# Products of zeros in TensorE's waits, from the attention's end to the first gather

## The chip, the core and the metric

The kernel runs on one core of a Trainium2 chip. A core has TensorE (PE, with its weight loads shown apart as PEld), VectorE (DVE), ScalarE (ACT), GpSimd (POOL) and SyncE (SP), which issues transfers. Each engine executes its own instructions in order, and semaphores tie the engines together. The metric is the device time of one execution in microseconds. TensorE's clock has two levels, 1.2 and 2.4 GHz; the profile gives the granted clock as a share, 0.50 or 1.00.

## The reference

Causal attention by blocks of 64 over 8 batches, 8 heads, 576 positions of width 64; then a layer of 8 experts, in which each of the 4608 tokens goes to one expert and each expert takes 576; then a dense layer with the activation h cos(h).

```python
attn = softmax(mask(q @ k.T / 8)) ; x = (attn @ v) as 4608 x 512
logits = x @ w_gate                       # 4608 x 8
for idx in argsort(-logits.flatten()):    # best pair of token and expert first
    tok, e = idx // 8, idx % 8
    if token unassigned and counts[e] < 576: assigned[tok] = e
for e: out[assigned == e] = relu(x[mask] @ w1[e]) @ w2[e]
h = out @ w_in ; result = (h * cos(h)) @ w_out
```

## The kernel before

`attention` runs first: 64 heads in a software pipeline whose order on TensorE is written out by hand. It leaves the rows `xs` in HBM and the gate's logits `lg` in SBUF. Then `moe` takes the experts one after another. The greedy assignment is replayed without a sort: the expert that fills up first is found, with the value of its last token.

For the first of them nothing else can run yet, so this search is on the path. `search_pe` (L776 to L804) finds the threshold four bits at a time, in eight rounds. In a round VectorE compares each token's best logit with 16 thresholds (`compare`, `cm`, L774), in four pieces of 7, 9, 10 and 10 tiles; TensorE counts by expert in 36 products of 8 columns, one a tile (L787); VectorE compares the counts with the capacity (`fl`, L789); one product with `W16` (L792) tells all partitions; and VectorE makes the next thresholds (L801, L803). Then `close` (L862 on) ranks the tokens of the expert: running sums and two products (L880, L881), one-hot matrices (`om`, `B`, `hot`, L891 to L903), 36 products that place the token numbers (L913) and one that spreads them (L921). The result is `idx` (L928), which GpSimd uses to gather the rows in five indirect transfers (`xg`, L938).

`begin` and `xpose` start the first expert's products. `xpose` transposes a gathered tile on TensorE (L1013), ScalarE rounds it to `xth` (L1018), VectorE takes the rest, `xtl` (L1019). For the second tile both go in two halves, and the second half's `xth` waits for the first half's `xtl`. TensorE's first products (L1190) need both tiles. Meanwhile `load_raw` brings weights `wr`; the fourth to sixth are held until gathers have landed, by a one-element copy on VectorE (L972). ScalarE turns them into `wh` (L979), VectorE into `wl` (L980). The claims of the second expert (L702 to L737: `sel`, `e`, `oh`, `w`, `cmp`, `cmw`, `ri`, `rj`, `rd`) run on VectorE at the same time.

The order of TensorE and VectorE is that of the program while the first search and close run; after that TensorE's is still that of the program, and the other engines' is set by a scheduler's model of costs. `wu` is a tile of zeros; products of it go into accumulators that nobody reads. Before, 14 of them (`warm`, L855) stand behind L921; transposes of `xg` whose result isn't read (L1022) follow the first two real ones.

Of the kernel before, what the change touches and what calls it, by code (L numbers as in the profile page):

```python
# [19 lines left out]
F32 = mybir.dt.float32  # L20
# [15 lines left out]
NT = 36  # L36
# [5 lines left out]
PR = dict(EC=3, E2=2, E5=7, GC=0, SI=1, NX=3, LV=3, Q0=2, WM=14, WE=0, SW=1, W0=16, WG=0, WN=5, PA=0, CS=2, sT=2, mx=3, tr=1, e32=3, RO=0, XO=0, SO=0, GO=200, TPS=4, SEP=5, L2=3, L5=9, LAG=3, WK=3, XG=5, BIG=16, GLD=99, IW=4, W1=14, CW=1, XS=6, AH=3)  # L42
# [11 lines left out]
def attention(ctx, tc, qk, vv, vt, cmask, wg, xs, lg, ident, wu, side, late):  # L54
# [5 lines left out]
    nc = tc.nc  # L60
# [4 lines left out]
    P = ctx.enter_context(tc.tile_pool(name="at_ps", bufs=1, space=PSUM))  # L65
# [386 lines left out]
    for g in range(NHD + 2):  # L452
        p, h = divmod(g, 2)
        b, pr = divmod(p, 4)
        on = g < NHD
        if on and b + 1 < B and g % 8 == (5 if b == 0 else PR["LV"]):
            if b == 0:
                hold(VB[1][0:1, 0, 0, 0:1])
                hold(VB[1][0:1, 4, 0, 0:1])
            load_v(b + 1)  # L460
        if g == 0:
            start()
            continue
        if on and h == 0 and p + 1 < NP:
            if p == 2:
                hold(VT[1][0:1, 0:1])
            load_vt(p + 1)
        if on and h == 0:
            if p > 1 and p + 3 < NP:
                load_max(p + 3)  # L470
            if p == 1:
                zero(0, nc.gpsimd)
                mask(0)
            if p > 3 and p + 2 < NP:
                load_raw(p + 2)
        work = side(g)
        gms = [x for x in MX.get(g, [g + 4]) if x < NHD]

        def m(u):
            for x in gms:  # L480
                mx_unit(x, u)

        def s(t):
            if on:
                sc_unit(g, t)

        def a(j):
            if 0 <= g - 1 < NHD:
                av_part(g - 1, j)

        def c():
            if h == 0 and 1 < p + 1 < NP and p != 1:
                crow(p + 1)

        def x1():
            if 0 <= g - 2 < NHD:
                sums(g - 2)

        def x2():
            if 0 <= g - 2 < NHD:  # L500
                norm(g - 2)
            if g % 8 == 2 and g > 2:
                store_x(b - 1)

        more = on and 0 < p and p + 1 < NP

        def rc():
            if more:
                copies(p + 1, h)

        def rd():
            if more:
                rests(p + 1, 0)

        def rp():
            if more:
                rests(p + 1, 1)

        def v():
            q = p + 1 if h == 1 and p + 1 < NP else None  # L520
            if q is not None:
                for j in range(5):
                    vg_unit(q, j)

        def k():
            for x in gms:
                if x % 2:
                    crow_max(x // 2)

        def V():  # L530
            for j in range(5):
                vg_unit(1, j)

        did = {"P0": lambda: rest_pair(1, 0), "P1": lambda: rest_pair(1, 1), "L3": lambda: load_max(3), "L4": lambda: load_max(4),
               "R0": lambda: row_part(1, 0, 4, 1), "R1": lambda: row_part(1, 4, 5, 1), "Y0": lambda: copies(1, 0), "Y1": lambda: copies(1, 1),
               "T0": lambda: round_pair(2, 0), "T1": lambda: round_pair(2, 1), "X0": lambda: head_max(0, NM[1]), "X1": lambda: head_max(1, NM[1]), "Z": lambda: zeros(2, nc.gpsimd), "Z1": fourth, "H6": lambda: load_raw(5), "C1": lambda: crow(1), "C": lambda: crow(2),
               "H": held, "H4": later_pair, "V": V, "x1": x1, "x2": x2, "c": c, "rc": rc, "rd": rd, "rp": rp, "v": v, "k": k}
        order = ORDER[h]
        if 0 < g < 4:
            order = (FIRST, SECOND, THIRD)[g - 1]  # L540
        if g == 6:
            order = order.replace(" c ", " c H6 ")
        if g > 59:
            order = LATE if g == 60 else LATE.replace("rd rp ", "")
            if g >= NHD:
                order = "x1 a0 a1 x2 D a2 a3 a4"
        for w in order.split():
            if w in did:
                did[w]()
            elif w[0] in "ABD":  # L550
                for f in work.pop(w[0], ()):
                    f()
            elif w[0] == "M":
                mx_unit(int(w[1]), int(w[2]))
            elif w[0] == "G":
                vg_unit(0, int(w[1]))
            elif w[0] in "sam" and len(w) == 2:
                {"s": s, "a": a, "m": m}[w[0]](int(w[1]))
        for w in work.values():
            for f in w:  # L560
                f()
        if g > 5:
            late()
    first.close()
    opening.close()
    store_x(B - 1)
# [115 lines left out]
def moe(ctx, tc, ro, xs, hs, lg, w1h, w2h, winh, wouth, out, ident, jp):  # L682
    nc=tc.nc
    C=ctx.enter_context(tc.tile_pool(name="mo_c",bufs=1))
    W=ctx.enter_context(tc.tile_pool(name="mo_w",bufs=2))
    P=ctx.enter_context(tc.tile_pool(name="mo_ps",bufs=4,space=PSUM))
# [3 lines left out]
    hp, asg, oh, w4, mc, sel, eid, idx, wu, e2 = (ro.hp, ro.asg, ro.oh, ro.w4, ro.mc, ro.sel, ro.eid, ro.idx, ro.wu, ro.e2)  # L690
# [70 lines left out]
    def last_base(je):  # L761

        jf=R.tile([128,1],F32,name="jf",bufs=1); f8=R.tile([128,8],F32,name="f8",bufs=1)
        V.tensor_reduce(jf,je,axis=AX.X,op=OP.max)
        V.scalar_tensor_tensor(f8,je,jf,rev8,op0=OP.is_equal,op1=OP.mult)
        fm=first(f8)
        V.tensor_scalar(jj,jf,-1.0,None,op0=OP.add)
        V.tensor_tensor(bx,bx,jj,op=OP.bitwise_xor)
        return fm
# [5 lines left out]
    def search_pe():  # L775
        for l in range(8):  # L776
            sh=28-4*l
            if l>0: compare(l,((0,7),(7,16),(16,26),(26,36)),th)
            cm=CM[l]
            if l>0: V.tensor_tensor(bx,bx,jj,op=OP.bitwise_xor)  # L780
            if l==2:
                XG[0,0]=W.tile([128,512],F32,name="xg",bufs=PR['XG'])
                G.indirect_dma_start(out=XG[0,0][0:16],out_offset=None,in_=xs,in_offset=bass.IndirectOffsetOnAxis(ap=T8[0:16,1,0:1],axis=0))
            yield
            ps=psum()
            for t in range(NT):
                nc.tensor.matmul(ps[0:16,0:8],lhsT=cm[:,t,:],rhs=oh[:,t,:],start=t==0,stop=t==NT-1)  # L787
            fl=R.tile([16,8],BF,name="fl")
            V.tensor_scalar(fl,ps[0:16,0:8],float(CAP),None,op0=OP.is_ge)  # L789
            yield  # L790
            ps2=psum()
            nc.tensor.matmul(ps2[:,0:8],lhsT=W16[:,l],rhs=fl,start=True,stop=True)  # L792
            if l==7: return last_base(ps2[:,0:8])
            if l==0:

                jf=R.tile([128,1],F32,name="jf",bufs=1)
                V.tensor_reduce(jf,ps2[:,0:8],axis=AX.X,op=OP.max)
                V.tensor_scalar(jj,jf,-float(1<<31),None,op0=OP.add)
                V.tensor_scalar(bx,jj,31,0x7FFFFFFF,op0=OP.arith_shift_right,op1=OP.bitwise_and)
            else:  # L800
                V.tensor_reduce(jj,ps2[:,0:8],axis=AX.X,op=OP.max)  # L801
            t2=R.tile([128,16],I32,name="th",bufs=2)
            V.scalar_tensor_tensor(t2,TS[:,l+1],jj[:,0:1],bx.to_broadcast([128,16]),op0=OP.bitwise_xor,op1=OP.bitwise_xor)  # L803
            th=t2.bitcast(F32)  # L804
# [43 lines left out]
        V.scalar_tensor_tensor(f8,ps[:,0:8],float(CAP),rev8,op0=OP.is_ge,op1=OP.mult)  # L848
        return first(f8)

    def warm(a,n):

        for _ in range(n):
            ps=P.tile([128,512],F32,name="acc",bufs=4)
            nc.tensor.matmul(ps[0:64],lhsT=a,rhs=wu,start=True,stop=True)  # L855

    sn=R.tile([128,1],F32,name="sn",bufs=1)
    XG={}
# [3 lines left out]
    def close(i,fm):  # L862
# [16 lines left out]
        ps=psum()  # L879
        nc.tensor.matmul(ps[:,0:72],lhsT=LT,rhs=g2f,start=True,stop=False)  # L880
        nc.tensor.matmul(ps[:,0:72],lhsT=ones,rhs=gs,start=False,stop=True)  # L881
        if i==0: warm(gs[:,0:64],PR['WE'])
        yield
        a2=R.tile([128,2,NT],F32,name="a2",bufs=1); pp=R.tile([128,NT],I32,name="pp",bufs=1); pi=R.tile([128,NT],I32,name="pi",bufs=1)
        V.scalar_tensor_tensor(a2,ps[:,0:72].rearrange("p (a t) -> p a t",a=2),-5000.0,g2,op0=OP.add,op1=OP.mult)
# [13 lines left out]
        hot=[]  # L899
# [11 lines left out]
        ps=psum()  # L911
        for t in range(NT):
            nc.tensor.matmul(ps[0:18,0:64],lhsT=B[:,t].rearrange("p s m -> p (s m)"),rhs=hot[t//9][:,t%9],start=t==0,stop=t==NT-1)  # L913
        yield
        pr=R.tile([18,2,64],BF,name="pr",bufs=1)
        V.tensor_copy(pr,ps[0:18,0:64].unsqueeze(1).to_broadcast([18,2,64]))
# [2 lines left out]
            yield from bank()  # L919
        ps=psum()  # L920
        nc.tensor.matmul(ps[:,0:9],lhsT=pr.rearrange("p h r -> p (h r)"),rhs=both,start=True,stop=True)  # L921
        if i==0: warm(hot[3][:,8],PR['WM'])
        yield
        m0=(CAP*i)//128; r0=9*i%2
        for h in range(2):

            c=(9*i+(h^r0))//2; b=h^r0; k=(10-b)//2
# [7 lines left out]
        for j in range(5):  # L935
            n=64 if (j==4 and i%2==0) else 128
# [201 lines left out]
    a,b,c=steps[-3:]  # L1138
# [178 lines left out]
```

## Time and profile before

| | |
|---|---|
| median of 3 runs | 1686.72 us (1684.54 to 1686.97) |
| the profiled execution | 1680.93 us |
| its span, first to last instruction | 1679.1 us |
| TensorE busy | 1655.2 us, 99% of the span |
| VectorE, ScalarE busy | 1084.7 us (65%), 808.7 us (48%) |
| mean granted clock | 0.990 |

Times in rows are microseconds from the span's start unless marked ns. A row of a timeline gives start, length, engine, line, operation, what is written and read, and in brackets the idle time before it and what ended that.

### The profile page before, as it was taken

Reading aid. Unit: us, or ns where it says so; the run is one execution under the profiler, and the core shown is the slowest. Engines: PE = TensorE matmul, PEld = TensorE weight load, DVE = VectorE, ACT = ScalarE, POOL = GpSimd, SP = SyncE. Lnnn points to the kernel's source line nnn. Section 1 sums busy time; section 2 is a strip of 40 time slices with the busy share of each in tenths; the row PEclk is TensorE's granted clock in tenths of the full one; section 3 lists DMA queues with packets and bytes.
Section 4 is the critical chain, followed back from the end, with each engine's and each line's share of the span. In section 5 each row is a group of like instructions: output and inputs, shape, how many; then the busy total and the mean of one; then the engine's idle time right before and its main releaser. Section 6 shows DMA issues by size and latency. Waiting matters only on the chain.

```text
span 1679.1 us, 29288 instructions
## 1 busy us (share of the span) xinstructions
PE 1655.2 (99%) x10852; PEld 1478.6 (88%) x10852; DVE 1084.7 (65%) x2896; ACT 808.7 (48%) x1622; POOL 294.2 (18%) x259
## 2 busy tenths in 40 slices
PE   9999999998899999999999999999999999999998
PEld 8999999997698898899889889988988988998887
DVE  6888888887769777676667667677554343433342
ACT  6566666664345634443442544344254344434443
POOL 7344443432124400100100100100110000000000
PEclk9999999998799999999999999999999999999999
DMA  8999999995442323323433423433433333323332
GB/s 165 284 231 230 245 251 241 235 206 181 144 155 107 120 95 108 122 96 95 130 87 103 122 88 102 132 89 104 119 120 94 98 104 95 102 83 97 113 107 82
DMA packets 108125, 230.24 MB, mean 137 GB/s; under 512 B 12637, under 2 KB 15251, under 8 KB 105955
## 3 DMA queue, kind: packets, MB, share of 16 engines
q1 hardware_dynamic: 92960, 191.21, 39.4%
q0 software_dynamic: 15024, 37.17, 9.9%
q8 instruction: 86, 1.41, 0.4%
q14 instruction: 55, 0.45, 0.1%
HBM read 192.52 MB, written 35.65 MB: 136 GB/s over the span
## 4 chain that ended last, share of the span: by engine, by line
PE 92%; issue 6%; DVE 1%; POOL 1%; ACT 0%; POOLq 0%; DVEq 0%
PE wk L1080 21%; PE acc L1105 21%; PE acc L1053 12%; PE av L288 10%; PE wk L1028 7%; PE acc L1028 4%; PE sT L239 3%; PE mx L169 3%; PE sT L240 3%; PE tr L271 2%; PE rt L1013 1%; PE rt L913 1%; PE wk L1190 1%; PE rt L787 1%; PE av L352 0%
## 5 line engine op out<-in xcount | busy, mean ns | idle before, releaser
L1105 PE MATMUL acc<-wh,big 128*128 128x512 f32 x1136 | 375.3, 392 | 0.0
L1105 PEld LDWEIGHTS acc<-wh,big 128*128 128x128 f32 x1136 | 212.6, 188 | 42.9
L1080 PE MATMUL wk<-yh,wh 128*128 128x512 f32 x576 | 227.8, 395 | 0.0
L288 PE MATMUL av<-vb,e 128*128 128x100 f32 (+1 forms) x1920 | 224.5, 259 | 0.0
L1080 PE MATMUL wk<-yl,wh 128*128 128x512 f32 x576 | 224.4, 390 | 0.0
L1080 PE MATMUL wk<-yh,win 128*128 128x512 f32 x576 | 224.3, 389 | 0.0
L1105 PE MATMUL acc<-wout,big 128*128 128x512 f32 x568 | 222.5, 392 | 0.0
L1083 ACT ACTIVATE big<-wk 128x512 int32<-128x512 f32 x144 | 85.8, 596 | 281.4 <-PE wk L1080 270.3
L1086 DVE SCALAR_TENSOR_TENSOR big<-big,wk 128x512 f32<-128x512 int32 x144 | 98.6, 684 | 186.8 <-ACT big L1083 186.8
L288 PEld LDWEIGHTS av<-vb,e 128*128 128x128 f32 (+1 forms) x1920 | 208.4, 173 | 4.1 <-ACT vb L275 0.2
L258 ACT ACTIVATE e<-sT 128x288 f32<-128x288 f32 (+3 forms) x320 | 132.2, 425 | 97.5 <-PE sT L240 89.7
L1053 PE MATMUL acc<-big,wh 128*128 128x288 f32 x1024 | 179.1, 297 | 0.0
L176 DVE TENSOR_REDUCE nm<-mx 128x1 f32<-128x288 f32 (+1 forms) x374 | 144.1, 428 | 51.3 <-PE mx L169 48.0
L980 DVE TENSOR_TENSOR wl<-wr,wh 128x512 fp32r<-128x512 f32 x128 | 88.1, 690 | 108.2 <-PE acc L1053 38.0
L1114 POOL DMA_INDIRECT out<-big,idx x36 | 35.7, 992 | 681.3 <-ACT big L1111 673.5
L1053 PEld LDWEIGHTS acc<-big,wh 128*128 128x128 f32 x1024 | 149.8, 189 | 0.1
L1091 DVE TENSOR_TENSOR big<-wk,big 128x512 f32<-128x512 f32 x144 | 99.2, 689 | 78.1 <-ACT big L1088 77.8
L979 ACT ACTIVATE wh<-wr 128x512 fp32r<-128x512 f32 x128 | 80.9, 633 | 106.6 <-DMA wr<-in_w 43.6
L239 PE MATMUL sT<-qk 128*128 128x288 f32 (+5 forms) x384 | 128.2, 343 | 0.5 <-ACT qk L220 0.2
L1080 PEld LDWEIGHTS wk<-yh,win 128*128 128x128 f32 x576 | 108.1, 188 | 23.0
L1080 PEld LDWEIGHTS wk<-yh,wh 128*128 128x128 f32 x576 | 108.4, 188 | 21.1
L1080 PEld LDWEIGHTS wk<-yl,wh 128*128 128x128 f32 x576 | 108.3, 188 | 21.1
(255 smaller groups left out, 3096.8 us busy)
## 6 DMA issues: line engine op xcount, KB each, us to landing
wh<-hs SPq DMA_DIRECT2D x256, 256.0 KB, 2.6
wr<-in_w SPq DMA_DIRECT2D x128, 256.0 KB, 2.6
R<-in_qk SPq DMA_DIRECT2D x30, 576.0 KB, 8.1
qk<-in_qk POOLq DMA_DIRECT2D x29, 576.0 KB, 8.1
vT<-in_vt SPq DMA_DIRECT2D x32, 288.0 KB, 7.6
w<-in_win SPq DMA_DIRECT2D x16, 512.0 KB, 6.6
ws<-w SPq DMA_DIRECT2D x32, 256.0 KB, 6.0
xs<-X SPq DMA_DIRECT2D x8, 1024.0 KB, 8.3
```

What stands on the lines that cost most here:

```text
L176: RED.append(nc.vector.tensor_reduce(m[:, c:c + 1], ps[:, o:o + n], axis=AX.X, op=OP.max))
L239: nc.tensor.matmul(out, lhsT=a[0:r, 1, h, k], rhs=a[0:r, 0, h, 64 + q0:64 + q0 + n], start=True, stop=False)
L258: nc.scalar.activation(e[:, o:o + n], ps[:, 0:n], AF.Exp, scale=0.125)
L288: nc.tensor.matmul(AV[hg % 2][0:n, c, w], lhsT=E32[hg][:, q:q + n], rhs=v[:, (j * H + hd) * 73 - o + w.start:(j * H + hd) * 73 - o + w.sto ...
L980: V.tensor_sub(l,raw,h.bitcast(F32))
L1028: nc.tensor.matmul(ps[q][:,0:288],lhsT=w[:,128*d:128*d+128],rhs=x[:,d,288*q:288*q+288],start=d==0 and n==0,stop=d==3 and n==2)
L1053: nc.tensor.matmul(ps[q][:,0:288],lhsT=w[:,sl],rhs=x[:,288*q:288*q+288],start=f==0 and n==0,stop=f==7 and n==2)
L1080: nc.tensor.matmul(ps,lhsT=w[:,sl],rhs=y[:,d,:],start=d==0 and n==0,stop=d==3 and n==2)
L1083: A.activation(k,ps,AF.Copy,scale=1/(2*math.pi))
L1086: V.scalar_tensor_tensor(r,k,-2*math.pi,ps,op0=OP.mult,op1=OP.add)
L1091: V.tensor_tensor(r,ps,r,op=OP.mult)
L1105: nc.tensor.matmul(acc[t],lhsT=g[:,128*t:128*t+128],rhs=w,start=c==0 and n==0,stop=c==15 and n==2)
```

## The change

Products of zeros are added on TensorE at these places: 8 of 512 columns at the attention's end, into the pool `mx`; in each search round one of 256 columns ahead of L792's product and three of 512 behind it (eight in the last round); in all rounds but the first two of 128 columns inside the row of 36; 11 behind L881's product; one behind each nine of L913's 36; and 22 in the place of 14 behind L921's. `warm` now always takes its weights from `wu`, 64 columns wide.

```diff
--- before.py
+++ after.py
@@ -561,6 +561,9 @@
                 f()
         if g > 5:
             late()
+    ps = P.tile([128, 512], F32, name="mx", bufs=PR["mx"])
+    for _ in range(8):
+        nc.tensor.matmul(ps, lhsT=wu[:, :128], rhs=wu, start=True, stop=True)
     first.close()
     opening.close()
     store_x(B - 1)
@@ -785,11 +788,14 @@
             ps=psum()
             for t in range(NT):
                 nc.tensor.matmul(ps[0:16,0:8],lhsT=cm[:,t,:],rhs=oh[:,t,:],start=t==0,stop=t==NT-1)
+                if l>0 and t in (6,15): warm(1,128)
+            warm(1,256)
             fl=R.tile([16,8],BF,name="fl")
             V.tensor_scalar(fl,ps[0:16,0:8],float(CAP),None,op0=OP.is_ge)
             yield
             ps2=psum()
             nc.tensor.matmul(ps2[:,0:8],lhsT=W16[:,l],rhs=fl,start=True,stop=True)
+            warm(3 if l<7 else 8)
             if l==7: return last_base(ps2[:,0:8])
             if l==0:
 
@@ -848,11 +854,11 @@
         V.scalar_tensor_tensor(f8,ps[:,0:8],float(CAP),rev8,op0=OP.is_ge,op1=OP.mult)
         return first(f8)
 
-    def warm(a,n):
+    def warm(n,c=512):
 
         for _ in range(n):
             ps=P.tile([128,512],F32,name="acc",bufs=4)
-            nc.tensor.matmul(ps[0:64],lhsT=a,rhs=wu,start=True,stop=True)
+            nc.tensor.matmul(ps[0:64,0:c],lhsT=wu[:,0:64],rhs=wu[:,0:c],start=True,stop=True)
 
     sn=R.tile([128,1],F32,name="sn",bufs=1)
     XG={}
@@ -879,7 +885,7 @@
         ps=psum()
         nc.tensor.matmul(ps[:,0:72],lhsT=LT,rhs=g2f,start=True,stop=False)
         nc.tensor.matmul(ps[:,0:72],lhsT=ones,rhs=gs,start=False,stop=True)
-        if i==0: warm(gs[:,0:64],PR['WE'])
+        if i==0: warm(11)
         yield
         a2=R.tile([128,2,NT],F32,name="a2",bufs=1); pp=R.tile([128,NT],I32,name="pp",bufs=1); pi=R.tile([128,NT],I32,name="pi",bufs=1)
         V.scalar_tensor_tensor(a2,ps[:,0:72].rearrange("p (a t) -> p a t",a=2),-5000.0,g2,op0=OP.add,op1=OP.mult)
@@ -911,6 +917,7 @@
         ps=psum()
         for t in range(NT):
             nc.tensor.matmul(ps[0:18,0:64],lhsT=B[:,t].rearrange("p s m -> p (s m)"),rhs=hot[t//9][:,t%9],start=t==0,stop=t==NT-1)
+            if i==0 and t%9==8: warm(1,512 if t<NT-1 else 256)
         yield
         pr=R.tile([18,2,64],BF,name="pr",bufs=1)
         V.tensor_copy(pr,ps[0:18,0:64].unsqueeze(1).to_broadcast([18,2,64]))
@@ -919,7 +926,7 @@
             yield from bank()
         ps=psum()
         nc.tensor.matmul(ps[:,0:9],lhsT=pr.rearrange("p h r -> p (h r)"),rhs=both,start=True,stop=True)
-        if i==0: warm(hot[3][:,8],PR['WM'])
+        if i==0: warm(22)
         yield
         m0=(CAP*i)//128; r0=9*i%2
         for h in range(2):
```

The built program shows what stands where. On TensorE, at the end of a search round, before (`cm` is the comparison, `fl` the counts' verdict, `W_79` the constant that spreads it):

```order
L787 LDWEIGHTS cm
L787 MATMUL rt<-oh,cm 16x8
L792 LDWEIGHTS W_79
L792 MATMUL rt<-fl,W_79 128x8
L787 LDWEIGHTS cm
L787 MATMUL rt<-oh,cm 16x8
```

The same place now, up to the first of three like products; line numbers are higher by 3 and more:

```order
L790 LDWEIGHTS cm
L790 MATMUL rt<-oh,cm 16x8
L861 LDWEIGHTS wu
L861 MATMUL acc<-wu 64x256
L797 LDWEIGHTS W_79
L797 MATMUL rt<-fl,W_79 128x8
L861 LDWEIGHTS wu
L861 MATMUL acc<-wu 64x512
```

A product of zeros stands on either side of the round's last product, and the first of the next 36 has three ahead of it.

On VectorE, at the first transposes, before (`xtl` is the low part of the gathered rows, `wr` the copy that holds a weight's load, `e`, `oh`, `w` the second expert's claims):

```order
L972 COPY wr<-xg 1x1
L713 TENSOR_REDUCE e_102<-e_6081 128x36
L1019 TENSOR_TENSOR xtl<-acc,xth 128x4x128
L1019 TENSOR_TENSOR xtl<-acc,xth 128x2x128
L972 COPY wr<-xg 1x1 x2
L715 SCALAR_TENSOR_TENSOR e_102<-asg,e_102 128x36
L716 TENSOR_TENSOR oh<-e_6081,e_102 128x288
L1019 TENSOR_TENSOR xtl<-acc,xth 128x2x128
L721 TENSOR_TENSOR e_6081<-oh,pw 128x288
```

The same place now:

```order
L716 TENSOR_REDUCE e_102<-e_6238 128x36
L718 SCALAR_TENSOR_TENSOR e_102<-asg,e_102 128x36
L979 COPY wr<-xg 1x1 x2
L719 TENSOR_TENSOR oh<-e_6238,e_102 128x288
L724 TENSOR_TENSOR e_6238<-oh,pw 128x288
L726 TENSOR_REDUCE w_90<-e_6238 128x72
L1026 TENSOR_TENSOR xtl<-acc,xth 128x4x128
L733 TENSOR_TENSOR cmw<-cmp,w_90 128x216
L1026 TENSOR_TENSOR xtl<-acc,xth 128x2x128
L736 TENSOR_REDUCE ri<-cmw 128x6
L739 TENSOR_TENSOR rj<-ri,fmask 128x24
L1026 TENSOR_TENSOR xtl<-acc,xth 128x2x128
```

The three `xtl` of the first two gathered tiles have moved behind the copies for the third gather and behind the claims' `oh`, `e` and `w`.

On ScalarE at the same place, before (`xth` is the high part of the gathered rows, `wh` a weight's, `big` the first products' output):

```order
L907 ACTIVATE sn<-asg 128x1
L1018 ACTIVATE xth<-acc 128x4x128
L1018 ACTIVATE xth<-acc 128x2x128 x2
L979 ACTIVATE wh<-wr 128x512
L1192 ACTIVATE big<-wk 128x256
```

The same place now:

```order
L913 ACTIVATE sn<-asg 128x1
L1025 ACTIVATE xth<-acc 128x4x128
L1025 ACTIVATE xth<-acc 128x2x128
L986 ACTIVATE wh<-wr 128x512
L1025 ACTIVATE xth<-acc 128x2x128
L986 ACTIVATE wh<-wr 128x512
L1199 ACTIVATE big<-wk 128x256
```

The fourth weight's `wh` has moved between the two halves of the second tile's `xth`, and the fifth's ahead of the first `big`. SyncE's and GpSimd's orders are as before.

## Rows read from the trace of the kernel before

**Rows 1.** The page, parts 1 and 2: busy time, and granted clock in slices.

```profile
PE 1655.2 (99%) x10852; PEld 1478.6 (88%) x10852; DVE 1084.7 (65%) x2896; ACT 808.7 (48%) x1622; POOL 294.2 (18%) x259
...
PEclk9999999998799999999999999999999999999999
```

**Rows 2.** Stretches: length, busy time (count) by engine, granted clock, DMA share, GB/s.

```profile
404.00:406.00 2.00, 0.17 (x3) 0.10 (x2) 1.82 (x8) 0.78 (x4) 0.00 (x0) 1.00 0.27 104
...
406.00:408.00 2.00, 1.28 (x37) 1.09 (x36) 1.21 (x6) 0.35 (x2) 0.91 (x4) 0.59 0.53 201
...
412.00:414.00 2.00, 0.92 (x31) 0.75 (x29) 1.24 (x8) 0.00 (x0) 0.98 (x1) 0.50 0.93 322
...
434.00:436.00 2.00, 2.00 (x7) 0.77 (x5) 1.93 (x6) 0.01 (x1) 1.69 (x2) 0.50 0.09 20
...
436.00:438.00 2.00, 2.00 (x8) 0.80 (x6) 1.38 (x4) 0.00 (x0) 1.39 (x3) 0.73 0.64 236
```

**Rows 3.** TensorE's timeline, 404 to 440: start, length, what, idle time before.

```profile
413.96 1.10 PE L787 MATMUL rt<-oh,cm 128*16 128x8 bf16 x36 [0.84 <-DVE cm L774]
...
426.77 0.22 PE L880 MATMUL rt<-g,LT 128*128 128x72 bf16 x1 [1.90 <-DVE g L872]
...
430.10 2.36 PE L913 MATMUL rt<-hot,B 128*18 128x64 bf16 x36 [2.77 <-DVE hot L903]
...
432.95 5.23 PE L855 MATMUL acc<-wu,hot 128*64 128x512 bf16 x14
```

**Rows 4.** Groups by line, TensorE, 404.5 to 433: busy, mean ns, idle.

```profile
L787 PE MATMUL rt<-oh,cm 128*16 128x8 bf16 x288 | 8.9, 167 | 8.5 <-DVE cm L774 6.2 <-DVE e L711 2.2
```

**Rows 5.** VectorE's timeline, a search round and the close.

```profile
413.63 0.96 DVE L774 TENSOR_TENSOR cm<-mc,th 128x112 bf16<-128x112 f32 x4
...
429.20 2.83 DVE L903 TENSOR_TENSOR hot<-iob,pc 128x576 bf16<-128x576 bf16 x5
```

**Rows 6.** TensorE's timeline around an inserted small product, L815.

```profile
451.32 0.31 PE L1190 MATMUL wk<-xth,wh 128*128 128x320 f32 x1
...
451.61 0.31 PE L1190 MATMUL wk<-xth,wl 128*128 128x320 f32 x1
...
451.76 0.19 PE L815 MATMUL rt<-rd,ones 128*128 128x24 bf16 x1
...
452.03 0.31 PE L1190 MATMUL wk<-xtl,wh 128*128 128x320 f32 x1
```

**Rows 7.** VectorE's timeline, 438 to 443.

```profile
438.84 0.14 DVE L972 COPY wr<-xg 1x1 f32<-1x1 f32 x1 [1.43 <-DMA xg<-xs,idx]
...
439.48 1.15 DVE L1019 TENSOR_TENSOR xtl<-acc,xth 128x512 fp32r<-128x512 f32 x2
...
440.87 0.46 DVE L716 TENSOR_TENSOR oh<-e,e 128x288 bf16<-128x288 f32 x1
...
441.25 0.42 DVE L1019 TENSOR_TENSOR xtl<-acc,xth 128x256 fp32r<-128x256 f32 x1
...
441.58 0.45 DVE L721 TENSOR_TENSOR e<-oh,pw 128x288 f32<-128x288 bf16 x1
...
442.06 0.45 DVE L723 TENSOR_REDUCE w<-e 128x72 bf16<-128x288 f32 x1
```

**Rows 8.** ScalarE's timeline, 440 to 444.

```profile
440.66 0.38 ACT L1018 ACTIVATE xth<-acc 128x256 fp32r<-128x256 f32 x1 [0.49 <-DVE wr L972]
...
443.09 0.63 ACT L979 ACTIVATE wh<-wr 128x512 fp32r<-128x512 f32 x1 [2.05 <-DMA wr<-in_w]
...
443.63 0.37 ACT L1192 ACTIVATE big<-wk 128x256 fp32r<-128x256 f32 x1
```

**Rows 9.** TensorE's timeline, the product that waits for the low half.

```profile
441.72 0.39 PE L1190 MATMUL wk<-xtl,wh 128*128 128x256 f32 x1
```

**Rows 10.** GpSimd's timeline, the third gather; and all gathers' landing.

```profile
436.55 1.13 POOL L938 DMA_INDIRECT xg<-xs,idx  x1 [0.30 <-issue]
...
DMA to landing us min/median/max: 3.5/3.7/6.0
```

## The prediction

> **What bounds the kernel now.** I read the page first: TensorE is busy 99% of the span, and the granted clock shows one dent, in the tenth and eleventh of its forty slices [rows 1]. The reader is to see that nearly the whole kernel runs at TensorE's pace, so a time lost ahead of the first expert is lost for good, and that only some 30 us are in question. Second, the busy time of short stretches [rows 2]: in 404 to 406 TensorE does 0.17 us of 2.00, after the attention's last products; in 406 to 408 the granted clock is 0.59 on the mean, then 0.50, the lower level (1.2 GHz), until after 434 to 436; in 436 to 438 it comes back, after a stretch of 14 products of zeros. Third, TensorE's timeline [rows 3] and the grouped lines of 404.5 to 433 [rows 4]: this is a chain of small steps between VectorE and TensorE. A search round holds 36 products of 8 columns in 1.10 us, with a hole of 0.84 us ahead that VectorE ends. Fourth, the timelines of VectorE and ScalarE from 438 to 444 [rows 7 to 10], where the gathered rows are split for the first expert's products.
>
> Is the chain paced by the clock? 1.10 us less one product's own 0.17 [rows 3, 4] is 0.93 us for 35 steps, 27 ns a step, while 8 columns at 1.2 GHz take 6.7 ns. So a round's pace is not that of the columns, and a faster clock has little to shorten. In the close, the 36 products of L913 take 2.36 us, of 64 columns each, 53 ns at 1.2 GHz, and there the clock does count; but their last operand comes from five VectorE instructions that run from 429.20 to 432.03 [rows 5], and the products end at 430.10 + 2.36 = 432.46 [rows 3], 0.43 us later. At most some 0.2 us can go there, since 4 products and one drain remain after 432.03.
>
> The Trainium skill ("TensorE: Matmul & The Clock Gate", section "Terms") prices a slow clock as the throttled time times the missing share of the pulses. By that, some 30 us at 0.50 would have cost 15 us, and the change would gain up to that. This case's rows disagree: in those 30 us TensorE's products are mostly not column-bound, by the 27 ns above.
>
> **The change part by part.** The sum goes against the profiled execution, 1680.93 us (span 1679.1); the median of the three runs, 1686.72, lies 5.79 us higher, and I carry the difference over.
>
> (1) *Eight products after the attention.* 8 x 512 columns at 2.4 GHz are 1.7 us. The first search product waits 2.2 us for VectorE's `e` of L711 [rows 4], and they lie in that wait. Cost nothing; if the clock were low they would take 3.4 us and cost 1.2 us.
>
> (2) *Products at the holes of the search.* After L792's product come three of 512 columns: 0.64 us at 2.4 GHz, against a hole of 0.84 us [rows 3]: nothing lost. The one of 256 columns ahead of L792 (0.11 us) lies beside VectorE's `fl`, which holds L792 up anyway. The two of 128 columns stand inside the row of 36, behind tiles 6 and 15, in seven rounds. There the cover is thin: VectorE makes the four pieces of `cm` in 0.96 us [rows 5], TensorE starts behind the first and catches up with it by only hundredths of a microsecond, since its 36 steps of 27 ns nearly fill the 1.10 us. Before shows no such insertion in this row. Lower bound: the 53 ns of streaming less about 20 ns of wait each, 0.03 us. Upper bound: the nearest inserted small product, L815: two steps take 0.29 us without it (451.32 to 451.61) and 0.42 with it (451.61 to 452.03), 0.13 us more [rows 6], though it has only 24 columns; with the longer streaming, 0.17 us. I take 0.07 us each, nearer the first, as the weights are half as wide as L815's: 7 x 2 x 0.07 = 1.0 us, between 0.4 and 2.4.
>
> (3) *Fills of the close.* Eight products behind the last L792 (1.7 us) lie in a hole of 1.90 us, eleven (2.4 us) in one of 2.77 [rows 3]. Those between L913's nine-tile groups lie in waits for VectorE. Nothing lost while the clock is high; L913 and the shorter drains give back 0.15 us.
>
> (4) *22 products instead of 14 ahead of the transposes.* 22 x 0.213 is 4.7 us, where 14 took 5.23 up to the clock's rise [rows 3]. They end about as before. Nothing by themselves.
>
> (5) *What moved on VectorE and ScalarE.* This is the largest term. The order of before lets VectorE make the low halves of the gathered rows (`xtl`, 0.42 us for a half, so some 0.7 for a whole) about as soon as ScalarE has the high ones: two from 439.48, the third at 441.25 [rows 7]. Now they stand behind the copy that waits for the third gather, then `oh`, L721 and L723 of the next expert's claims. ScalarE takes the conversion of the fourth raw weight (`wh`) before the second half of `xth` of the second gather; before, after it. All times here leave the shift of (2) out.
>  The VectorE side: the third gather, issued at 436.55, lands some 3.5 us later, about 440.1 [rows 10]; two copies take 0.2, then `oh`, L721 and L723 follow at 0.48 us each, as L723 follows L721 [rows 7], to 441.75; then the first `xtl`, to 442.4, L730, and the second, to about 442.9.
>  The ScalarE side: `wh` waited for its transfer until 443.09 [rows 8]; this transfer is held until the second gather has landed (438.84 [rows 7]), so it can't come earlier. With the next instruction 0.54 us behind (443.09 to 443.63 [rows 8]), the second half of `xth` starts at 443.63, not at 440.66. The later of both sides decides: 443.63. It takes 0.38, `xtl` then 0.42, and the product that needs it starts at 443.63 + 0.38 + 0.03 + 0.42 + 0.05 = 444.51 instead of 441.72 [rows 9]: 2.8 us. Behind it TensorE has no hole in which to make this good beyond small ones: I count 0.25 us of stalls between the following groups as won. So 2.55 us, between 2.0 and 3.1. A queue behind the waiting instruction: on ScalarE the rest of the split and all `big` outputs of the first steps; TensorE waits for these.
>
> SyncE and GpSimd issue the same instructions in the same order; their loads and gathers shift with the index, no more.
>
> Sum: 0 + 1.0 - 0.15 + 0 + 2.55 = 3.4 us. 1680.93 + 3.4 = 1684.3 for the profiled execution, and with the 5.79 1690.1 us against the median, 0.20% slower.
>
> **The rivals.** *The clock falls in spite of the fill.* No stretch of before looks like the new search: 404 to 406, nearly empty, was followed by the fall; the attention and all that comes later are nearly full at the high level. The new rounds lie between, nearer the full side, but all products there have few columns or half the array. If it falls early: three products of 512 columns take 1.28 us against 0.84, the two of 128 another 0.3, together 0.7 us a round, 4.9 us in seven; eight take 3.4 against 1.90 us (+1.5), eleven up to 4.7 against 2.77 (+1.2, as they raise the clock on the way, like those of 434 to 436 did). With (5): 7.6 + 2.55 = 10.2 us, 1696.9.
>
> *Not slower.* The products of 128 columns hide in the waits for `cm` after all, at 0.03 us or less each, and the weight's transfer lands by 442.4, so that VectorE's side, 442.9, decides instead of 443.63. Then 0.4 - 0.15 + 1.8 = 2.1 us: 1688.8, within 0.2%. It decides at a sum of 3.4 us. For it: the transfer shared the queues with three gathers; against: it is issued after the same landing as before and meets the same gathers.
>
> *Faster: the columns pace the cold stretch.* The rule cited above asks for this. If L787's 8.9 us of products [rows 4] and L913's 2.3 halved, 5.6 us would go, and with (5) and (2) the sum would be -2.2 us or, should (5) be hidden, up to -5. 1684.5 and below. Against it stand the 27 ns a step and VectorE's 0.96 us for `cm`, which no TensorE clock changes: a round could end at most some 0.2 us earlier.
>
> **How the numbers follow.** Forecast as summed 0.60, its own range 1688.8 to 1691.6; the clock falls 0.20; not slower 0.14; faster 0.06. About 0.2%, 3.4 us, is what a measurement of this kernel can tell from no change; the forecast stands on that line. Slower by more: half of 0.60 plus a little as the upper bounds reach farther than the lower ones (0.34), and all of the 0.20: 0.54. Within: 0.26 + 0.14 = 0.40. Faster by more than 0.2%: 0.06. The range of 8 in 10 reaches from 1686.7 (bounds of (2) and (5) both low, median noise of 1 us) to 1697.5, into the fallen clock.
>
> **What would show it.** Granted clock 1.00 in each stretch from 404 to 440 shows (1) to (3) right; 0.50 in the search is the first rival. A round, from one L792 product to the next, was 2.35 us: 2.5 shows (2). The search's L787 steps still at some 25 ns show that the clock didn't pace them. In (5) ScalarE's `wh` stands before the second half of `xth`, and TensorE idles for about 3 us between the fifth and eighth products of the first expert; if this wait is under 1 us, (5) is wrong. A kernel at or below 1686 us would prove the main reasoning wrong.

## The result and the profile after

The changed kernel takes 1698.92 us (median of 6 runs, 1697.52 to 1702.22), the kernel before, beside it, 1683.61 us: ratio 1.0091, interval 1.0075 to 1.0108, 15.3 us slower. A second set of runs gave 1.0105 (1.0088 to 1.0122). The forecast was 1690.1, 3.4 us slower, and its range ended at 1697.5.

The profiled execution of the changed kernel took 1702.22 us, with a span of 1698.3. Lines from L787 on have higher numbers now: L787 is L790 (the row of 36), L792 is L797, L880 is L886, L921 is L928, L1019 is L1026, L1018 is L1025, L979 is L986, L1190 is L1197, L1028 is L1035. Every product of zeros ahead of the transposes is L861.

The page, parts 1 and 2, against [rows 1]:

```profile
PE 1681.6 (99%) x10934; PEld 1489.6 (88%) x10934; DVE 1085.3 (64%) x2896; ACT 809.1 (48%) x1622; POOL 294.2 (17%) x259
...
PEclk9999999998799999999999999999999999999999
```

VectorE, ScalarE and GpSimd do what they did; TensorE has 82 more products and 26.4 us more busy time; the dent in the clock is still there. The stretches, columns as in [rows 2] (TensorE's busy time first, the granted clock third from the end):

```profile
412.00:414.00 2.00, 1.46 (x14) 0.69 (x14) 1.61 (x9) 0.00 (x0) 0.13 (x1) 1.00 1.03 373
414.00:416.00 2.00, 2.00 (x35) 1.38 (x35) 0.76 (x5) 0.00 (x0) 0.00 (x0) 0.71 1.04 229
416.00:418.00 2.00, 2.00 (x22) 0.90 (x21) 1.07 (x6) 0.00 (x0) 1.03 (x1) 0.50 0.93 294
434.00:436.00 2.00, 2.00 (x37) 1.19 (x36) 0.71 (x4) 0.00 (x0) 0.00 (x0) 0.50 0.00 0
...
442.00:444.00 2.00, 2.00 (x17) 0.95 (x15) 2.00 (x5) 1.94 (x4) 0.00 (x0) 0.96 0.34 121
...
461.00:463.00 2.00, 2.00 (x13) 2.00 (x12) 0.61 (x2) 0.98 (x2) 0.00 (x0) 0.59 0.00 0
```

The clock stays at 1.00 through the first row of 36 and falls to 0.50 at 414.8, in the second (1.00 from 414.0 to 414.7, 0.50 from 414.9 on), although TensorE is busy there without a break. It comes back at 442. Then it falls a second time, from 459.2 to 462.6, which the one trace of the kernel before doesn't show.

TensorE's timeline, the first two rounds with fills and the start of the third, against [rows 3]:

```profile
412.17 0.16 PE L797 MATMUL rt<-fl,W 16*128 16x8 bf16 x1
412.26 0.83 PE L861 MATMUL acc<-wu 128*64 128x512 bf16 x3
413.55 0.32 PE L790 MATMUL rt<-oh,cm 128*16 128x8 bf16 x7 [0.45 <-DVE cm L777]
413.80 0.24 PE L861 MATMUL acc<-wu 128*64 128x128 bf16 x1
413.97 0.38 PE L790 MATMUL rt<-oh,cm 128*16 128x8 bf16 x9
...
415.38 0.18 PE L797 MATMUL rt<-fl,W 16*128 16x8 bf16 x1
415.50 1.49 PE L861 MATMUL acc<-wu 128*64 128x512 bf16 x3
416.92 0.33 PE L790 MATMUL rt<-oh,cm 128*16 128x8 bf16 x7
...
417.42 0.38 PE L790 MATMUL rt<-oh,cm 128*16 128x8 bf16 x9
...
418.91 0.18 PE L797 MATMUL rt<-fl,W 16*128 16x8 bf16 x1
```

A round was 2.35 us. The first one with fills takes 415.38 - 412.17 = 3.21 (2.73 without), the next 418.91 - 415.38 = 3.53. In the first, at 1.00 but for its last 0.6 us, the three products of 512 end with 0.45 us of wait for `cm` left: this hole costs nothing, as forecast. In the second they take 1.49 us where the hole was 0.84, and nothing waits for `cm` any more. The steps of the row themselves don't change: nine in 0.38 us at 413.97 (clock 1.00) and at 417.42 (0.50).

The rest of TensorE's stretch, to the first expert's products:

```profile
436.62 3.62 PE L861 MATMUL acc<-wu 128*64 128x512 bf16 x8
440.17 0.24 PE L886 MATMUL rt<-g,LT 128*128 128x72 bf16 x1
...
446.63 0.17 PE L928 MATMUL rt<-both,pr 18*128 18x9 bf16 x1
446.74 4.93 PE L861 MATMUL acc<-wu 128*64 128x512 bf16 x22
...
456.88 0.39 PE L1197 MATMUL wk<-xtl,wh 128*128 128x256 f32 x1 [2.73 <-DVE xtl L1026]
...
459.40 0.58 PE L1197 MATMUL wk<-xth,wh 128*128 128x256 f32 x1 [1.66 <-ACT xth L1025]
459.86 0.58 PE L1197 MATMUL wk<-xtl,wh 128*128 128x256 f32 x1
```

And what the two stalls wait for, on VectorE ([rows 7] before), then on ScalarE ([rows 8] before):

```profile
452.55 0.14 DVE L979 COPY wr<-xg 1x1 f32<-1x1 f32 x1 [1.35 <-DMA xg<-xs,idx]
...
456.41 0.42 DVE L1026 TENSOR_TENSOR xtl<-acc,xth 128x256 fp32r<-128x256 f32 x1
```

```profile
458.44 0.63 ACT L986 ACTIVATE wh<-wr 128x512 fp32r<-128x512 f32 x1 [4.73 <-DMA wr<-in_w]
458.98 0.37 ACT L1025 ACTIVATE xth<-acc 128x256 fp32r<-128x256 f32 x1
```

The first stall, 2.73 us, is VectorE's: its low halves come behind `oh`, `e` and `w`, and the second of them ends at 456.83 (456.41 + 0.42), 0.05 us before TensorE goes on. The second, 1.66 us, is ScalarE's: `wh` waits for its weight until 458.44, and the second half of `xth` behind it.

To compare kernels I cut each trace at four TensorE rows: the first `fl,W` product, the last one, the `both,pr` product (L921 before) and the first group of L1028 (L1035 in the changed kernel). What follows the last cut takes 1226.8 to 1226.9 us in all thirteen traces, so all of the difference lies ahead of it; what lies ahead of the first cut varies between executions: it is 407.5 to 409.3 us in eight traces and 410.0 to 412.7 in five, and in these five, that of the changed kernel among them, the clock fell once inside the attention, for 3.4 or 6.8 us (near 64 or at 346.6), where all kernels are alike. In us, with the difference to before:

```
                      search         close          split          sum    ratio measured
before                16.83           8.12          19.49           -      1
changed kernel        24.34 +7.51    10.12 +2.00    24.90 +5.41   +14.9    1.0091
changed, second trace 24.48 +7.65     9.53 +1.41    25.75 +6.26   +15.3    1.0105
x1_close22            16.83  0.00     9.82 +1.70    21.42 +1.93    +3.6    1.0023
x2_full14             24.48 +7.65     9.52 +1.40    20.41 +0.92   +10.0    1.0062
x3_close14            16.83  0.00     9.86 +1.74    19.37 -0.12    +1.6    1.0005
x4_close18            16.83  0.00     9.22 +1.10    22.52 +3.03    +4.1    1.0009
y1_no_inner14         20.61 +3.78    10.07 +1.95    20.73 +1.24    +7.0    1.0035
y2_wide14             23.69 +6.86     9.03 +0.91    20.25 +0.76    +8.5    1.0049
y3_one14              16.83  0.00     8.44 +0.32    19.20 -0.29     0.0    1.0011
y4_wide_no_inner14    20.42 +3.59     9.96 +1.84    20.57 +1.08    +6.5    1.0031
z1_before22           16.82 -0.01     8.13 +0.01    21.64 +2.15    +2.2    1.0025
z2_inner_only         21.01 +4.18     8.12  0.00    19.71 +0.22    +4.4    1.0027
```

A ratio of 1.0010 is 1.7 us. The sums of single traces and the ratios agree within 2.6 us. They compare with one trace of the kernel before, of a fast execution (1680.93; its medians beside the runs were 1682.2 to 1684.6).

### The profile page after: what moved, and what is told of

The parts are those of the page before. It is cut to its first block, busy times and chain, and to the rows that moved or that the text cites. A ratio compares the mean times of both kernels' runs of the same rounds, so it can differ in the third digit from the quotient of the medians.

```text
span 1698.3 us, 29451 instructions
## 1 busy us (share of the span) xinstructions
PE 1681.6 (99%) x10934; PEld 1489.6 (88%) x10934; DVE 1085.3 (64%) x2896; ACT 809.1 (48%) x1622; POOL 294.2 (17%) x259
## 4 chain that ended last, share of the span: by engine, by line
PE 86%; issue 8%; DMA 4%; POOL 1%; ACT 1%; DVE 1%; SPq 0%; POOLq 0%; DVEq 0%; ACTq 0%
PE wk L1087 21%; PE acc L1112 21%; PE acc L1060 12%; PE av L288 9%; PE wk L1035 7%; PE acc L1035 4%; PE sT L239 3%; PE mx L169 3%; PE sT L240 2%; PE tr L271 2%; DMA qk<-ct 1%; PE rt L1020 1%; DMA X<-in_qk 1%; PE wk L1197 1%; PE rt L919 0%
## 5 line engine op out<-in xcount | busy, mean ns | idle before, releaser
L986 ACT ACTIVATE wh<-wr 128x512 fp32r<-128x512 f32 x128 | 80.8, 633 | 109.3 <-DMA wr<-in_w 48.0
```

## The experiments

Theory after the result: the clock falls in spite of the fills (the first rival), and the loss is what no longer fits at 0.50, plus the new order of VectorE and ScalarE. Against it: the fills cost by their place, whatever the clock; or the 22 products by themselves.

**x1_close22**: the changed kernel with the search as before.

```
-                if l>0 and t in (6,15): warm(1,128)
-            warm(1,256)
-            warm(3 if l<7 else 8)
+            if l==7: warm(8)
```

> The changed kernel without the products of zeros in the search rounds (the eight behind the last round, those of the close and the 22 stay). Theory (the search's fill costs 7.5 us at the low clock, the order behind 22 products 4.4 and a second fall of the clock 1.1): rounds back at 2.35 us, the eight still cost 1.6 us, the stall ahead of the first expert stays: 7 us slower than before. Rival (the order costs nothing; what the trace of the change shows there is a slow transfer of one execution): within 2.5 us of before. Rival (the search's fill is hidden, the close's costs all): as the change, 15 us slower.

Measured 1686.63 us, ratio 1.0023 (1.0012 to 1.0035). Its timelines of TensorE and ScalarE:

```profile
424.40 3.62 PE L859 MATMUL acc<-wu 128*64 128x512 bf16 x8
...
444.21 0.39 PE L1195 MATMUL wk<-xtl,wh 128*128 128x256 f32 x1 [2.54 <-DVE xtl L1024]
```

```profile
443.71 0.63 ACT L984 ACTIVATE wh<-wr 128x512 fp32r<-128x512 f32 x1 [2.48 <-DVE xtl L1024]
```

That is 3.9 us (2.0 to 5.9), between the theory's 7 and the rival's 2.5. Two things cost: the eight products, at 0.50, take 3.62 us in a hole of 1.90 (+1.7), and TensorE waits 2.54 us for `xtl`. The trace puts ScalarE's `wh` down to VectorE's `xtl`, but the weight landed just then too (about 443.6, 3.3 us behind its issue), so which of the two it waited for can't be told. The clock comes back at 429.4, after 5 us in which TensorE did nothing but products of zeros and two of the close's: products of zeros can bring it back.

**x2_full14**: the changed kernel with 14 products behind L928, so that VectorE's and ScalarE's orders are those of before.

```
-        if i==0: warm(22)
+        if i==0: warm(14)
```

> The changed kernel with 14 instead of 22 products ahead of the transposes; VectorE's and ScalarE's orders are then those of before. Theory: the stall of 4.4 us and the low clock of 1.1 us after it go, the search's 7.5 and the close's 2 stay: 9.5 us slower than before. Rival (the order costs nothing): 15 us slower, as the change.

1691.97 us, ratio 1.0062 (1.0044 to 1.0080). The search keeps its 24.5 us and the granted clock its fall (0.50 from 409.6 to 436.9); the split comes back to 0.9 us over before. So some 10 us belong to the fills, as the theory had it (9.5), and the rest hangs on the 22.

**x3_close14** and **x4_close18**: x1 with 14 and with 18 products (the diff is x3's; x4 has 18 in its place). With 18 only VectorE's `xtl` has moved; ScalarE takes both halves of `xth` ahead of the weight, as before.

```
-        if i==0: warm(22)
+        if i==0: warm(14)
```

> The changed kernel without the search's products of zeros and with 14 ahead of the transposes: only the attention's end and the close are filled, VectorE's and ScalarE's orders are those of before. Theory: 1.6 us for the eight at the low clock, nothing else: 1 to 2 us slower than before. Rival (the close's fill brings the clock up earlier and this pays): 0.5 to 1 us faster.

> As the run before it, with 18 products ahead of the transposes: VectorE's three xtl stand behind the copies for the third gather and interleaved with oh, e and w, but ScalarE takes both halves of the second tile's xth ahead of the fourth weight, as before the change. Theory (two parts: VectorE's order alone puts the second half some 1.4 us later, ScalarE's wait for the weight the rest): 1.4 us slower than with 14, and 3 to 4 us faster than with 22. Rival (VectorE's order is all of it): as with 22.

x3: 1683.11 us, 1.0005 (0.9990 to 1.0020), which excludes neither its theory nor its rival. x4: 1684.74 us, 1.0009 (0.9997 to 1.0020), with a single trace that shows more, +4.1; of that, 1.4 us lie behind the product of [rows 9], where the clock fell once more, from 446.4 to 449.8. In that trace TensorE and ScalarE wait for VectorE's `xtl`:

```profile
444.94 0.39 PE L1195 MATMUL wk<-xtl,wh 128*128 128x256 f32 x1 [1.84 <-DVE xtl L1024]
```

So VectorE's order alone makes TensorE wait 1.84 us. By the runs, 14 to 18 costs 0.0004 and 18 to 22 another 0.0014, but the intervals overlap. The traces, one of each, say more: from the `both,pr` product to that of [rows 9] it is 8.72 us in x3, 10.55 in x4 and 10.99 in x1, so VectorE's order has 1.8 us of the price there and ScalarE's some 0.4.

**z1_before22**: the kernel before, with `WM=22` in place of `WM=14` and no other edit.

> The kernel before with 22 products of zeros instead of 14 behind L921 and nothing else of the change: no fills, the orders of VectorE and ScalarE those of the changed kernel. The search and the close keep their 16.8 and 8.1 us at the lower clock. If the order of VectorE and ScalarE is the cost by itself, as the run with all fills of the close and 22 products says (+2.1 us up to the product that takes the low half, 1.0023), it comes at +2 to +4 us, 1.0012 to 1.0025, and TensorE waits 2 to 4 us more between L921's product and that one. If the cost came of the fills of the close together with the order, it stays within 1 us of the kernel before (1.0000 to 1.0006).

1686.96 us, 1.0025 (1.0015 to 1.0034). TensorE, VectorE and ScalarE:

```profile
436.86 6.28 PE L855 MATMUL acc<-wu,hot 128*64 128x512 bf16 x22
...
446.99 0.38 PE L1190 MATMUL wk<-xtl,wh 128*128 128x256 f32 x1 [1.42 <-DVE xtl L1019]
...
447.97 0.39 PE L1190 MATMUL wk<-xtl,wh 128*128 128x256 f32 x1
```

```profile
442.82 0.14 DVE L972 COPY wr<-xg 1x1 f32<-1x1 f32 x1 [1.49 <-DMA xg<-xs,idx]
...
446.51 0.42 DVE L1019 TENSOR_TENSOR xtl<-acc,xth 128x256 fp32r<-128x256 f32 x1
```

```profile
446.55 0.63 ACT L979 ACTIVATE wh<-wr 128x512 fp32r<-128x512 f32 x1 [1.42 <-DMA wr<-in_w]
```

Search and close are untouched, the split is 2.15 us longer (the runs say 4.2, 2.5 to 5.7; what makes up the rest isn't in the split of this trace). The run changes the number of products and the order together. Here the clock is at 0.50 when the 22 begin, so they end 1.0 us later behind L921 than 14 did (6.28 us against 5.23). The trace still puts the time down to the order: TensorE then waits another 1.42 us for VectorE's second `xtl`, which ends at 446.93 (446.51 + 0.42) and comes as late behind L921 as in the changed kernel (10.18 and 10.20 us), where the 22 end earlier. So in this order fewer products would, by the trace, only have made TensorE wait longer; 22 products in the old order were not run. The weight lands 3.7 us behind the second gather (446.55 against 442.82; 4.25 in the kernel before).

**z2_inner_only**: the kernel before with only the two products of 128 columns in seven rows.

```
+                if l>0 and t in (6,15): warm(1,128)
```

> The kernel before with only the two products of 128 columns inside seven rows of 36 (14 behind L921, no products in the holes, none of 256 columns, none in the close, none behind the attention). If an inserted product costs 0.3 us in the row at the lower clock wherever it stands (row of 36 1.99 us in the changed kernel against 1.35): rounds of 2.9 to 3.0 instead of 2.35 and +4.2 us, 1.0025. If it costs only because the overfilled hole let TensorE start the row late, behind VectorE's cm, rounds stay within 0.15 of 2.35 and the sum is +1 us or less (1.0006). As the prediction sized it, 0.07 us each: +1.0 us.

1687.70 us, 1.0027 (1.0015 to 1.0039). One of its rounds on TensorE, all at 0.50:

```profile
419.94 0.33 PE L787 MATMUL rt<-oh,cm 128*16 128x8 bf16 x7 [0.84 <-DVE cm L774]
420.19 0.31 PE L856 MATMUL acc<-wu 128*64 128x128 bf16 x1
...
420.75 0.32 PE L856 MATMUL acc<-wu 128*64 128x128 bf16 x1
420.99 0.65 PE L787 MATMUL rt<-oh,cm 128*16 128x8 bf16 x20
421.89 0.16 PE L793 MATMUL rt<-fl,W 16*128 16x8 bf16 x1 [0.24 <-DVE fl L790]
```

The hole is still 0.84 and the wait for `fl` still 0.24, and each row is 0.60 us longer: 0.30 us an inserted product, none of it hidden, 14 x 0.30 = 4.2 us, as the expectation's first case had it. The price doesn't come from the overfilled hole.

**y1_no_inner14**: x2 without those two products.

```
-                if l>0 and t in (6,15): warm(1,128)
```

> All fills with 14 ahead of the transposes, but without the two products of 128 columns inside each row of 36. Theory (at the low clock an inserted product costs 0.3 us, so 0.6 us a round, and the three behind L792's product overfill their hole by 0.53): clock low again, rounds of 2.9 us instead of 3.5, 5.2 us slower than before, half of the 10.4 with them. Rival (the inner ones hide in the waits for cm, as the lower bound of the prediction had it): still 10 us slower.

1690.12 us, 1.0035 (1.0020 to 1.0050), 5.9 us where the theory had 5.2. One of its rounds ends late, then a usual one:

```profile
413.84 0.16 PE L796 MATMUL rt<-fl,W 16*128 16x8 bf16 x1 [0.61 <-DVE fl L793]
...
416.69 0.18 PE L796 MATMUL rt<-fl,W 16*128 16x8 bf16 x1
416.80 1.49 PE L860 MATMUL acc<-wu 128*64 128x512 bf16 x3
418.21 1.05 PE L790 MATMUL rt<-oh,cm 128*16 128x8 bf16 x36
...
419.55 0.18 PE L796 MATMUL rt<-fl,W 16*128 16x8 bf16 x1
```

2.86 us instead of 2.35: the three products of 512 columns cost 0.51 us a round at 0.50. The product of 256 is hidden: from the row's start to the next `fl,W` product it is 419.55 - 418.21 = 1.34 us, as in before (1.10 of row and 0.24 of wait). The round that ends at 413.84 is an exception of 3.54 us, in which `fl` came late; y4 has one of 3.60. Why is not known; it makes 0.7 of this trace's +3.78.

**y2_wide14**: x2 with fills on all 128 columns of the array; **y4_wide_no_inner14**: the same without the two inner products.

```
-            nc.tensor.matmul(ps[0:64,0:c],lhsT=wu[:,0:64],rhs=wu[:,0:c],start=True,stop=True)
+            nc.tensor.matmul(ps[:,0:c],lhsT=wu[:,0:128],rhs=wu[:,0:c],start=True,stop=True)
```

> All fills with 14 ahead of the transposes, every product of zeros with 128 columns of weights instead of 64, as those at the attention's end have: as long, but on the whole array. Theory (nearly all of the cost comes from the clock's fall, as 512 columns take 0.43 us instead of 0.21): if it stays at 1.00, the hole's three fit, the inner two cost 0.24 us each as in the first filled round, 7 x 0.48 = 3.4 us, the close nothing: 3.4 us slower than before; if it falls, 10 us slower. Rival (the products cost as such, whatever the clock): 10 us slower with the clock at 1.00.

> As the run before it, without the two products inside the row of 36. Theory (search and close aren't paced by the clock): if the clock stays at 1.00, rounds of 2.35 us as at 0.50 and within 1 us of before; if it falls, as with narrow weights, 5.2 us slower. Rival (a search at the full clock is faster): with the clock at 1.00, 4 to 6 us faster than before.

y2: 1693.09 us, 1.0049 (1.0031 to 1.0068). y4: 1690.26 us, 1.0031 (1.0018 to 1.0044). A stretch of y2:

```profile
412.00:414.00 2.00, 2.00 (x32) 1.20 (x29) 0.78 (x6) 0.00 (x0) 0.00 (x0) 0.71 1.03 216
```

The clock falls here too, in the second row of 36 (y2: at 412.8), and the loss is nearly that of the same fills on half of the array (x2 for y2, y1 for y4). That only half of the array was used is not what let the clock fall.

**y3_one14**: fills cut so that each fits its hole at 0.50: one of 512 in a round, four behind the last, six in the close, 14 behind L928.

```
-                if l>0 and t in (6,15): warm(1,128)
-            warm(1,256)
-            warm(3 if l<7 else 8)
+            warm(1 if l<7 else 4)
-        if i==0: warm(11)
+        if i==0: warm(6)
-        if i==0: warm(22)
+        if i==0: warm(14)
```

> Fills cut to what fits at the low clock: one product of 512 columns behind L792's product, none inside the row of 36 and none ahead of L792, four behind the last round, six behind L887's place, 14 ahead of the transposes. Theory: 0.43 us fits in 0.84, 1.7 in 1.90, 2.6 in 2.77: within 0.5 us of before, clock low through the search. Rival (each filled round costs something whatever its length): 3 us slower.

1685.97 us, 1.0011 (0.9999 to 1.0024). Its first rounds:

```profile
411.09 0.16 PE L795 MATMUL rt<-fl,W 16*128 16x8 bf16 x1 [0.32 <-DVE fl L792]
...
413.82 0.16 PE L795 MATMUL rt<-fl,W 16*128 16x8 bf16 x1 [0.24 <-DVE fl L792]
413.91 0.63 PE L859 MATMUL acc<-wu 128*64 128x512 bf16 x1
414.82 1.11 PE L790 MATMUL rt<-oh,cm 128*16 128x8 bf16 x36 [0.27 <-DVE cm L777]
416.17 0.16 PE L795 MATMUL rt<-fl,W 16*128 16x8 bf16 x1 [0.25 <-DVE fl L792]
```

```profile
411.00:413.00 2.00, 1.02 (x21) 0.64 (x21) 1.61 (x9) 0.00 (x0) 0.05 (x1) 1.00 1.02 367
```

Each product ends 0.27 us ahead of `cm`, and the search's rounds are those of before, against the rival; the runs alone, 1.9 us slower (-0.2 to 4.0), wouldn't exclude its 3 us. The round from 411.09 to 413.82 runs almost whole at 1.00 and takes 2.73 us; the same round of the kernel before ran at 0.50 and took 2.73 (407.88 to 410.61). The higher level bought nothing in this round.

**z3_again**: the changed kernel once more.

> The changed kernel once more, unaltered, for a second trace of its gathers and its weight transfer beside these two. If the 13.2 us from L928's product to the one that takes the low half belonged to the traced execution (the weight's transfer landed 5.8 us behind the second gather, 4.25 in the kernel before), it is 11 us here (+2.1) and the second stretch at the lower clock may be missing, with a time some 2 to 3 us below the first trace's 1702. If it belongs to the changed kernel, it is 13 us again. The ratio should be 1.008 to 1.010 either way.

1699.08 us, 1.0105. The split was no accident of the first trace (ScalarE's and TensorE's timelines):

```profile
453.72 0.63 ACT L986 ACTIVATE wh<-wr 128x512 fp32r<-128x512 f32 x1 [4.35 <-DMA wr<-in_w]
```

```profile
452.52 0.39 PE L1197 MATMUL wk<-xtl,wh 128*128 128x256 f32 x1 [2.72 <-DVE xtl L1026]
...
454.67 0.58 PE L1197 MATMUL wk<-xth,wh 128*128 128x256 f32 x1 [1.29 <-ACT xth L1025]
```

Both stalls are back, the product of [rows 9] starts 12.8 us behind L928's (13.2 in the first trace, 8.9 before), and the clock falls again, from 453.8 to 460.7.

## Why the prediction was wrong

The direction was right. The likeliest case and its size were not: of the 14.9 us that the trace of the changed kernel shows, 9.5 lie in search and close, for which that case had 1.0 - 0.15. By the prediction's steps:

- *The premise of the 0.60 case*, that the clock holds, is the step that failed first: with it fall the "nothing lost" of the holes in (2) and (3). The first rival came true, in the second row of 36. No kernel tried kept the clock at 1.00 through the search, with fills on half of the array or all of it.
- *(1)* right: between the eight products and the row, TensorE only waits 0.37 us; they cost nothing.
- *(2)* failed in a second way that doesn't hang on the clock: the inserted products, put at 0.07 us each, cost 0.24 at 1.00 (first filled round: 3.21 - 2.73 = 0.48 for two) and 0.30 at 0.50 (z2). I had taken L815 as the upper end, 0.17 [rows 6], but that one stands between products of 320 columns, while here each neighbour takes some 27 ns. So the forecast would have been some 7 x 0.48 - 1.0 = 2.4 us short even had the clock held. The three of 512 do fit at 1.00, and cost 0.51 us a round at 0.50 (y1).
- *The first rival's price* was 4.9 us for the search; measured 7.5, of which the inserted products 4.2 (z2; it had 0.15 us for each, not 0.30) and the overfilled holes the rest, 3.3 (y1 and y4 have 3.6 to 3.8, with 0.7 to 0.8 in one late round). The eight were right: +1.5 forecast, +1.6 measured from the last `fl,W` product to L886 (3.66 against 2.06). The eleven's +1.2 didn't come: the close from L886 on is 6.46 us in the changed kernel against 6.06, and 5.86 in its second trace.
- *(3)* its 0.15 us come back where the clock is up before the row of L919 starts: 5.86 us in the second trace is 0.2 below before. Its eight and eleven stood under the premise that failed.
- *(4)* right in the changed kernel, where the clock is up again: 22 products end in 4.93 us. From 0.50 they take 6.28 (z1).
- *(5)* right that the order costs, and near in size (2.55 against 2.15, z1). In z1, set back to the times of before by the `both,pr` product, VectorE's second `xtl` ends at 443.0 (forecast 442.9) and the product of [rows 9] starts at 444.05 (forecast 444.51, before 441.72). ScalarE's weight came 0.5 us sooner than in before, though (5) held that it can't come earlier. Wrong is where TensorE waits: not about 3 us between the fifth and eighth products, but ahead of the second, for VectorE's moved `xtl` (z1, x1, x4 and both traces of the changed kernel). Between the fifth and eighth it waits 0.2 us in z1, and by (5)'s own sign, under 1 us, (5) would be wrong there; only in the changed kernel it is 1.66 and 1.29, behind ScalarE's wait for the weight. There the split costs 5.4 and 6.3 us. Of that, 2.15 is the order; the weight lands 5.9 and 5.5 us behind the second gather instead of 3.7 in z1, about 2 more; and the second fall of the clock takes the rest: in [rows 9]'s terms, from that product to the first group of L1028 it is 11.67 us (459.86 to 471.53) where it was 10.60.
- *What no term of the prediction had:* the late weight goes with the filled search. It is issued 0.3 us behind the second gather's copy in every trace; `wh` starts 5.0 to 5.9 us behind that copy in the six traces with all or nearly all of the search's fills (both of the changed kernel, x2, y1, y2, y4), 3.6 to 4.5 in the seven others. With the old order too (x2, y1, y2, y4) the split is then 0.8 to 1.2 us longer, where x3, y3 and z2 have -0.3 to +0.2.
- *The rival on the columns*, and with it the rule of the Trainium skill cited there ("TensorE: Matmul & The Clock Gate", section "Terms"), is refuted for the search: nine steps take 0.38 us at either level, and y3's round is 2.73 us at either. Where products have more columns the level does show. Nine of L913's, of 64, take 0.64 us at 0.50 and 0.43 at 1.00 (y3, at 433.21 and 434.17), but most of that lies beside VectorE's `hot`, and the close won 0.2 us by it, as (3) says. In the split, with 256 columns, it is 0.58 us for the product at 459.86 against 0.39 in [rows 9].

Added up: 4.2 (inserted products) + 3.3 (holes) + 2.0 (close) + 2.2 (order) + 3.2 (late weight and second fall) = 14.9 us, the sum of the traces, against 15.3 measured.

Open: why the weight's transfer takes longer behind a filled search; why y1 and y4 have a late round; what 22 products cost in the old order; and what would keep the clock at 1.00 in this search. That the fills were zeros is not by itself the reason, since in x1 it came back behind little else. No kernel run is faster than the one before; y3, x3 and x4 can't be told from it.

## What to carry to other kernels

Before filling an engine's waits to win back its clock, look whether the steps take the same time at both levels; if they do, there is next to nothing to win (here 0.2 us, in the close), and a fill must fit its hole at the lower level, because the clock may fall all the same. A small product put into a row of very short ones cost its whole insertion here, 0.24 to 0.30 us, whatever the row waits for elsewhere. And where an order comes out of a planner that counts the fills as work, read the other engines' orders too: a number changed on TensorE moved VectorE's and ScalarE's work by 2 us.

## What was not expected of the hardware

A TensorE that the trace shows busy through whole 2 us stretches (416 to 418, and 434 to 436, in the changed kernel) was granted 0.50 all the same. An inserted product of 128 columns between products of 8 took 0.24 us at 1.00 and 0.30 at 0.50, more than four times the 53 ns and almost three times the 107 ns of its columns at those levels. In both traces of the changed kernel the clock fell again, for 3.4 and 6.8 us, where TensorE had waited 2.7 us, worked through five products and was waiting another 1.3 to 1.7. The length of a stall doesn't tell the cases apart: x4 lost it for 3.4 us, 1.5 us behind a single stall of 1.84, while x1, with one of 2.54, and z1, with one of 1.42, kept it.
